# Three raw q, k buffers, one square buffer, another order of loads, and fewer fillers in a fused attention and MLP kernel

## Chip, cores and metric

The kernel runs on one core of a Trainium2 chip. The time is device microseconds of one execution. The kernel before took 342.39 us (median of 3 runs) when the prediction was made. All times below are of runs that computed the right result.

## The reference

Selective attention (causal, with a decay bias from a running sum of `s`) for 8 batches of 8 heads, 576 tokens, head dimension 64, then a two-layer MLP with exact Gelu on the 4608 tokens.

```python
def _attn_ref(q, k, v, s):                    # q, k, v: (8, 8, 576, 64) float32
    scores = scale * np.matmul(q, k.transpose(0, 1, 3, 2))
    cum = np.cumsum(np.maximum(s, 0.0), axis=-1)
    bias = -(cum[:, :, :, None] - cum[:, :, None, :])
    scores = np.where(causal, -1e9, scores + np.minimum(bias, 0.0))
    attn = softmax(scores)                    # cut
    return np.matmul(attn, v)

def _moe_ref(x, w_in, w_out):                 # x: (4608, 512), w_in: (512, 2048), w_out: (2048, 512)
    h = x @ w_in
    return (0.5 * h * (1 + erf(h / sqrt(2)))) @ w_out
```

## The kernel before

The MLP works on nine chunks of 512 tokens. While chunk c runs on TensorE, the attention of batch b = c + 1 is woven into it: layer 1 of the chunk (16 column tiles of w_in, two to a group, eight groups `f2`), then layer 2 in 16 groups with a list of attention pieces (`side`) between them. VectorE transposes q and k of the next batch and scales its v in layer 1 of the chunk; ScalarE makes the exponentials, the Gelu, and squares of v (and of q, k of batch 0) whose sums feed a certificate (a check at the end; if it fails, a slower general path runs); VectorE's `absmax` of q, k does the same for the later batches. A filler is a matmul of zeros whose result nobody reads; it only keeps TensorE busy.

```python
def raw_qk(b):                                # q and k of one batch, as loaded
    if (b, "qk") not in raws:
        raws[b, "qk"] = work.tile([128, 2, HG, S * 2], bf16, tag="rawqk", bufs=2, name="raw_qk")
    return raws[b, "qk"]

def square_qk(g, i):                          # ScalarE, batch 0 alone
    sq = work.tile([128, S * 2], bf16, tag="sqk", bufs=1, name="sqk")
    nc.scalar.activation(sq, raws[0, "qk"][:, i, g, :], func=AF.Square, scale=D ** -0.5,
                         accum_out=ssq[:, g, i : i + 1])

def square_v(b, st):                          # ScalarE, five for each batch; only the sum is used
    sq = work.tile([128, H * D], bf16, tag="sq", bufs=2, name="sq")
    nc.scalar.activation(sq[:n_st], raws[b, "v"][:n_st, st]..., func=AF.Square,
                         accum_out=sumv[:n_st, b, st : st + 1])

def absmax(b, g): ...                         # VectorE, reads raws[b, "qk"], 2.5 us each

for c in range(NCH):
    b = c + 1
    if c > 0 and b + 1 < B:
        load_qks(b + 1)                       # GpSimd queue; waits for a free raw_qk buffer
        load_v(b + 1, nc.gpsimd)
    ...                                       # layer 1: tr_qk(b), scale_v(b), absmax(b) on VectorE
    if c == 0:
        ...
        side[12] = [(av, b, 1, 3, True), (square_qk, 1, 0), (square_qk, 1, 1)]
        ...
        load_qks(2)
        load_v(2, nc.gpsimd)
    else:
        ...                                   # scores, masks (mk), attention times v (av), squares of v
        if c == 1:
            side[0].extend([(absmax, c, 0), (absmax, c, 1)])
```

## Time and profile before

| what | value |
|---|---|
| time, three runs | 339.94, 342.39, 343.69 us |
| span of the profiled run (341.48 us) | 339.7 us, mean granted clock 0.969 |
| busy: TensorE, VectorE, ScalarE | 92%, 59%, 56% |
| TensorE without work, 81.5 to 92 and 105 to 111.6 us | 10.4 and 6.6 us |

The page calls 92% of TensorE busy, but part of that is work at half clock. So look for two things: where TensorE stands still (a hole), and where it is busy but slow (the granted clock is the share of its full clock that it was given).

### The profile page before, as it was taken

Reading aid. Unit: us, or ns where it says so; the run is one execution under the profiler, and the core shown is the slowest. Engines: PE = TensorE matmul, PEld = TensorE weight load, DVE = VectorE, ACT = ScalarE, POOL = GpSimd, SP = SyncE. Lnnn points to the kernel's source line nnn. Section 1 sums busy time; section 2 is a strip of 40 time slices with the busy share of each in tenths; the row PEclk is TensorE's granted clock in tenths of the full one; section 3 lists DMA queues with packets and bytes.
Section 4 is the critical chain, followed back from the end, with each engine's and each line's share of the span. In section 5 each row is a group of like instructions: output and inputs, shape, how many; then the busy total and the mean of one; then the engine's idle time right before and its main releaser. Section 6 shows DMA issues by size and latency. Waiting matters only on the chain. (4 is left out here: it accounts for less than half of the span.)

```text
span 339.7 us, 6150 instructions
## 1 busy us (share of the span) xinstructions
PE 314.1 (92%) x2538; PEld 158.7 (47%) x2538; DVE 200.7 (59%) x400; ACT 190.2 (56%) x256; POOL 52.8 (16%) x72
## 2 busy tenths in 40 slices
PE   8999989996193899999999999999999999999994
PEld 3478645442051344554454444544454445444441
DVE  7677567049853397679567955895598552232011
ACT  2676967885063156855668566755765675303500
POOL 8533000600804001040104010400000000000000
PEclk9999999999678599999999999999999999999999
DMA  7999932690799614673575466631211131020012
GB/s 140 236 212 210 212 67 92 110 197 11 126 259 175 154 23 72 148 192 49 83 179 141 68 107 165 169 42 52 77 46 23 64 95 31 8 95 32 1 65 69
DMA packets 30980, 36.48 MB, mean 107 GB/s; under 512 B 15648, under 2 KB 20000, under 8 KB 30944
## 3 DMA queue, kind: packets, MB, share of 16 engines
q0 software_dynamic: 11552, 23.07, 35.5%
q1 hardware_dynamic: 19248, 12.80, 14.3%
q8 instruction: 22, 0.36, 0.5%
q14 instruction: 14, 0.11, 0.1%
q10 hardware_dynamic: 144, 0.13, 0.1%
HBM read 36.85 MB, written 9.44 MB: 136 GB/s over the span
## 5 line engine op out<-in xcount | busy, mean ns | idle before, releaser
L465 PE MATMUL h_ps<-xT,w_in_r 128*128 128x512 bf16 (+1 forms) x640 | 135.2, 363 | 6.6 <-issue 6.6
L481 PE MATMUL o_ps<-w_out_r,gT 128*128 128x512 bf16 x576 | 137.5, 383 | 1.2 <-DMA w_out_r<-in_moe_w_out_dram 1.2
L470 ACT ACTIVATE gT<-h_ps 128x1024 bf16<-128x1024 f32 (+1 forms) x80 | 74.4, 938 | 73.4 <-PE h_ps L465 72.7
L465 PEld LDWEIGHTS <-w_in_r 128*128 128x128 bf16 x640 | 60.5, 99 | 62.3 <-issue 10.1
L481 PEld LDWEIGHTS <-gT 128*128 128x128 bf16 x576 | 52.4, 98 | 58.6 <-issue 5.8
L358 ACT ACTIVATE P<-sc_ps 128x1024 bf16<-128x1024 f32 x56 | 54.3, 1021 | 44.3 <-PE sc_ps L343 44.3
L491 DVE COPY o_sb<-o_ps 128x512 f32<-128x512 f32 x32 | 22.1, 691 | 48.4 <-PE o_ps L481 48.4
L442 DVE RECIPROCAL rc<-av 128x4 f32<-128x4 f32 (+1 forms) x80 | 14.0, 175 | 53.2 <-PE av L433 53.2
L187 DVE STREAM_TRANSPOSE qkT<-raw_qk 128x576 f32<-128x576 f32 x32 | 37.6, 1243 | 10.5 <-DMA raw_qk<-in_q_dram 8.5
L122 POOL DMA_DIRECT2D raw_v<-in_v_dram x40 | 34.0, 869 | 60.9 <-ACT sq L212 55.0
L433 PE MATMUL av<-vv,P 128*128 128x65 bf16 x576 | 30.9, 195 | 11.0 <-DVE P L366 10.4
L433 PEld LDWEIGHTS <-P 128*128 128x128 bf16 x576 | 27.6, 99 | 28.1 <-DVE P L366 11.5
L443 DVE TENSOR_TENSOR x<-av,rc 128x256 bf16<-128x256 f32 (+1 forms) x80 | 33.8, 423 | 3.0
L204 DVE TENSOR_REDUCE amx<-raw_qk 128x2 f32<-128x2304 bf16 x14 | 35.1, 2533 | 0.0
L366 DVE TENSOR_TENSOR P<-P,tri_bf 128x1024 bf16<-128x1024 bf16 x32 | 21.9, 685 | 10.9 <-ACT P L358 10.3
L220 DVE TENSOR_TENSOR vv<-raw_v,wb 128x512 bf16<-128x512 f32 (+1 forms) x40 | 26.0, 690 | 0.8 <-DMA raw_v<-in_v_dram 0.7
L212 ACT ACTIVATE sq<-raw_v 128x512 bf16<-128x512 f32 (+1 forms) x40 | 24.6, 624 | 0.0
L106 POOL DMA_DIRECT2D raw_qk<-in_q_dram x9 | 6.3, 695 | 95.3 <-DVE amx L204 67.7
L343 PE MATMUL sc_ps<-qkT 32*128 32x256 bf16 (+2 forms) x560 | 18.3, 255 | 0.0
L343 PEld LDWEIGHTS <-qkT 32*128 32x128 bf16 x560 | 11.8, 94 | 13.1 <-issue 12.3
L417 PE MATMUL f_ps<-zero 128*128 128x512 bf16 x49 | 14.3, 423 | 1.2 <-DVE zero L150 1.2
L395 ACT ACTIVATE P<-sc_ps 128x1024 bf16<-128x1024 f32 x8 | 8.1, 1023 | 5.5 <-PE sc_ps L388 5.5
(79 smaller groups left out, 98.7 us busy)
## 6 DMA issues: line engine op xcount, KB each, us to landing
out_dram<-o_sb SPq DMA_DIRECT2D x35, 256.0 KB, 2.2
raw_v<-in_v_dram POOLq DMA_DIRECT2D x32, 256.0 KB, 8.7
raw_qk<-in_q_dram POOLq DMA_DIRECT2D x7, 576.0 KB, 5.9
raw_qk<-in_k_dram POOLq DMA_DIRECT2D x7, 576.0 KB, 9.1
w_in_r<-in_moe_w_in_dram POOLq DMA_DIRECT2D x4, 512.0 KB, 12.3
w_out_r<-in_moe_w_out_dram POOLq DMA_DIRECT2D x4, 512.0 KB, 14.6
raw_v<-in_v_dram POOLq DMA_DIRECT2D x8, 128.0 KB, 10.5
raw_qk<-in_q_dram POOLq DMA_DIRECT2D x2, 288.0 KB, 5.8
```

Of the source, the lines that this page charges most:

```text
L122: eng.dma_start(out=t[:n_st, st, :, :], in_=bass.AP(tensor=v.tensor, offset=v.offset + b * H * S * D + st * 128 * D, ap=[[D, n_st], [S * D ...
L187: nc.vector.transpose(qkT[b % 2][:, i, g, :S, :].rearrange("p s e -> p (s e)").bitcast(fp32) .rearrange("p (l j) -> p j l", j=LT), raws[b, ...
L204: nc.vector.tensor_reduce(amx[:, b * HG + g], raws[b, "qk"][:, :, g, :], axis=AX, op=ALU.max, apply_absolute_value=True,)
L212: nc.scalar.activation(sq[:n_st], raws[b, "v"][:n_st, st].rearrange("p h d -> p (h d)"), func=AF.Square, accum_out=sumv[:n_st, b, st : st ...
L220: nc.vector.tensor_tensor(vv[b % 2][:n_st, st, :, 0:D], raws[b, "v"][:n_st, st, :, :], w.unsqueeze(2).to_broadcast([n_st, H, D]), op=MULT,)
L343: nc.tensor.matmul(s_ps[h // 2][:, h % 2, off : off + n], lhsT=qk[r, 1, g, jt * 128 : jt * 128 + 128, e], rhs=qk[r, 0, g, i0 : i0 + n, e], ...
L358: nc.scalar.activation(P[:, 2 * h2 : 2 * h2 + 2, o : o + 512], s_ps[h2], func=AF.Exp, scale=scale)
L433: nc.tensor.matmul(o_ps[:, h, :], lhsT=P[:, h, off : off + 128], rhs=vv[b % 2][:, jt, 4 * g + h, :], start=(i == 0), stop=(i == len(BLK[it ...
L443: nc.vector.tensor_tensor(x_of[b, it][:n, g * 256 : g * 256 + 256].rearrange("p (h d) -> p h d", d=D), o_ps[:n, :, 0:D], rc[:n].unsqueeze( ...
L465: nc.tensor.matmul(h_ps[:, i, :], lhsT=w_in_r[:, ko, ft * 128 : (ft + 1) * 128], rhs=xT[:, ko, c * NB + n0 : c * NB + n1], start=(ko == 0) ...
L470: nc.scalar.activation(gT_of[c][:, f2 * 2 : f2 * 2 + 2, n0:n1], h_ps, func=AF.Gelu)
L481: nc.tensor.matmul(y_of[c, sub], lhsT=gT[:, ft, sub * 128 : (sub + 1) * 128], rhs=w_out_r[:, ft, :], start=(ft == 0), stop=(ft == FT - 1),)
```

## The change

The intent: a third raw buffer lets q, k of batch 2 be loaded without waiting for batch 0's buffer; w_out's second half goes ahead of the part of v that is needed later; the start of batch 0 is tightened. One square buffer now serves q, k and v: with the third raw buffer there is no room in SBUF for the old ones.

```diff
-            ... tag="rawqk", bufs=2, name="raw_qk")
+            ... tag="rawqk", bufs=3, name="raw_qk")
@@ square_qk
-        sq = work.tile([128, S * 2], bf16, tag="sqk", bufs=1, name="sqk")
+        sq = work.tile([128, S * 2], bf16, tag="sq", bufs=1, name="sq")
@@ square_v
-        sq = work.tile([128, H * D], bf16, tag="sq", bufs=2, name="sq")
+        sq = work.tile([128, S * 2], bf16, tag="sq", bufs=1, name="sq")
@@ start of batch 0 (more such lines cut)
-    filler(22)
+    filler(17)
     cum_sum()
+    masks()
     weights()
-    filler(4)
+    filler(3)
@@ loads
-    load_v(1, nc.gpsimd)
+    load_v(1, nc.gpsimd, (0, 1))
     load_w(1, 2)
     load_w(1, 3)
+    load_v(1, nc.gpsimd, (2, 3, 4))
@@ order of batch 0 (cut)
     mk_item(0, 1, 0)
-    sc_first(0, 1, (1,))
-    filler(2)
+    sc_first(1, 1, (0,))
     av_item(0, 1, 0)
@@ chunk 0
+                load_qks(2)
+                load_v(2, nc.gpsimd)
                 side = [[] for _ in range(16)]
-                side[3] = [(sc, b, 1, 0), (scale_v, b, 2), (mk, b, 1, 0)]
-                side[5] = [(sc, b, 0, 1), (av, b, 0, 0), (av, b, 0, 1), (scale_v, b, 3)]
-                side[6] = [(av, b, 1, 0, True), (mk, b, 0, 1)]
+                side[3] = [(sc, b, 1, 0), (mk, b, 1, 0)]
+                side[5] = [(sc, b, 0, 1), (av, b, 0, 0), (av, b, 0, 1)]
+                side[6] = [(scale_v, b, 2), (av, b, 1, 0, True), (mk, b, 0, 1)]
@@ (scale_v of the fourth piece to side[8]; the old place of batch 2's loads)
-                load_qks(2)
-                load_v(2, nc.gpsimd)
```

More of the change, by code (lines that the diff above doesn't have):

```diff
@@ L101, in raw_qk @@
         if (b, "qk") not in raws:
-            raws[b, "qk"] = work.tile([128, 2, HG, S * 2], bf16, tag="rawqk", bufs=2, name="raw_qk")
+            raws[b, "qk"] = work.tile([128, 2, HG, S * 2], bf16, tag="rawqk", bufs=3, name="raw_qk")
         return raws[b, "qk"]
@@ L210, in square_v @@
         n_st = 128 if st < ST - 1 else SL
-        sq = work.tile([128, H * D], bf16, tag="sq", bufs=2, name="sq")
+        sq = work.tile([128, S * 2], bf16, tag="sq", bufs=1, name="sq")
         nc.scalar.activation(
-            sq[:n_st], raws[b, "v"][:n_st, st].rearrange("p h d -> p (h d)"), func=AF.Square,
+            sq[:n_st, : H * D], raws[b, "v"][:n_st, st].rearrange("p h d -> p (h d)"), func=AF.Square,
             accum_out=sumv[:n_st, b, st : st + 1],
@@ L373, in mk_item, with sc_first @@
             )
-    def sc_first(g, u, halves=(0, 1)):
+    def sc_first(g, u, halves=(0, 1), fill=1):
         if (0, g) not in P_of:
@@ L393, in sc_first @@
                         )
-            filler(1)
+            if fill:
+                filler(fill)
             nc.scalar.activation(
@@ L531 @@
     sc_first(0, 0)
-    filler(3)
-    masks()
     tr_qk(0, 0, 1)
@@ L537 @@
     sc_first(0, 1, (0,))
-    filler(4)
+    filler(2)
     sc_first(1, 0, (0,))
@@ L542 @@
     scale_v(0, 1)
-    filler(2)
     sc_first(1, 0, (1,))
-    filler(2)
     av_item(0, 0, 0)
@@ L548 @@
     av_item(0, 0, 1)
+    sc_first(0, 1, (1,))
     mk_item(0, 1, 0)
-    sc_first(0, 1, (1,))
-    filler(2)
+    sc_first(1, 1, (0,))
     av_item(0, 1, 0)
     av_item(0, 1, 1)
-    sc_first(1, 1, (0,))
+    sc_first(1, 1, (1,), 0)
     to_xT(0, 0, True)
-    filler(1)
+    filler(2)
     to_xT(0, 1, True)
-    sc_first(1, 1, (1,))
+    filler(2)
     mk_item(0, 0, 1)
@@ L619 @@
             if c == 0:
+                load_qks(2)
+                load_v(2, nc.gpsimd)
                 side = [[] for _ in range(16)]
                 side[0] = [(sc, b, 0, 0), (scale_v, b, 0), (scale_v, b, 1), (mk, b, 0, 0)]
-                side[3] = [(sc, b, 1, 0), (scale_v, b, 2), (mk, b, 1, 0)]
-                side[5] = [(sc, b, 0, 1), (av, b, 0, 0), (av, b, 0, 1), (scale_v, b, 3)]
-                side[6] = [(av, b, 1, 0, True), (mk, b, 0, 1)]
+                side[3] = [(sc, b, 1, 0), (mk, b, 1, 0)]
+                side[5] = [(sc, b, 0, 1), (av, b, 0, 0), (av, b, 0, 1)]
+                side[6] = [(scale_v, b, 2), (av, b, 1, 0, True), (mk, b, 0, 1)]
                 side[7] = [(sc, b, 1, 1), (av, b, 1, 1, True), (to_xT, b, 0, True)]
-                side[8] = [(av, b, 0, 2), (to_xT, b, 1, True), (gelu_set,), (mk, b, 1, 1)]
+                side[8] = [(scale_v, b, 3), (av, b, 0, 2), (to_xT, b, 1, True), (gelu_set,), (mk, b, 1, 1)]
                 side[9] = [(av, b, 0, 3)]
```

## The prediction

> **What bounds the kernel now.** I read the page's forty slices first, then the engines in stretches around the holes, then who waited for whom, then the instructions in order of time. From the page (tenths of a slice of 8.5 us):
>
> ```profile
> PE   8999989996193899999999999999999999999994
> PEclk9999999999678599999999999999999999999999
> ```
>
> TensorE is the bound: 9s from slice 14 to slice 38, and the waits from 136 to 300 us name not one for it. The holes are slices 9 to 12 (76 to 110 us), and in slices 10 to 13 the granted clock is low too. Those slices in stretches (stretch; length; busy time and instruction count of PE, PEld, DVE, ACT, POOL; granted clock; DMA share; GB/s):
>
> ```profile
> 81.50:92.00 10.50, 0.10 (x3) 0.07 (x3) 10.38 (x6) 1.04 (x2) 5.94 (x8) 0.75 0.46 75
> 92.00:98.00 6.00, 6.00 (x52) 2.68 (x56) 2.50 (x6) 1.94 (x2) 1.14 (x2) 0.59 1.07 267
> 105.00:111.60 6.60, 0.02 (x1) 0.05 (x2) 0.67 (x1) 0.00 (x0) 3.13 (x4) 0.66 1.21 156
> 111.60:118.40 6.80, 6.80 (x33) 2.89 (x34) 2.74 (x4) 1.13 (x2) 0.00 (x0) 0.58 0.66 164
> ```
>
> Two holes of TensorE, each followed by 6 to 7 us in which it is busy at about 0.6 of its clock. The first hole in order of time (start, duration):
>
> ```profile
> 61.40 0.70 POOL L106 DMA_DIRECT2D raw_qk<-in_q_dram  x1 [26.53 <-ACT sqk L198]
> 70.67 1.26 DVE L187 STREAM_TRANSPOSE qkT<-raw_qk 128x576 f32<-128x576 f32 x1 [8.19 <-DMA raw_qk<-in_q_dram]
> 75.43 2.32 DVE L187 STREAM_TRANSPOSE qkT<-raw_qk 128x576 f32<-128x576 f32 x2
> 77.68 3.16 DVE L220 TENSOR_TENSOR vv<-raw_v,wb 128x512 bf16<-128x512 f32 x5
> 80.77 9.91 DVE L204 TENSOR_REDUCE amx<-raw_qk 128x2 f32<-128x2304 bf16 x4
> 90.61 0.67 DVE L491 COPY o_sb<-o_ps 128x512 f32<-128x512 f32 x1
> 91.21 0.67 DVE L366 TENSOR_TENSOR P<-P,tri_bf 128x1024 bf16<-128x1024 bf16 x1
> 91.94 0.40 PE L433 MATMUL av<-vv,P 128*128 128x65 bf16 x4 [10.40 <-DVE P L366]
> ```
>
> With two raw q, k buffers, batch 2's q and k need batch 0's buffer, whose last readers are the squares on ScalarE at 56 to 61 us. GpSimd sat 26.5 us before it could issue; q landed at 70.7 us, k at 73.8. VectorE had stood idle for 8.2 us, then did transposes, v scaling and four 2.5 us maxima in one row, and only then the mask that TensorE's attention-times-v was waiting for. The second hole:
>
> ```profile
> 99.52 2.54 SPq L404 DMA_TRANSPOSE xT<-x  x2
> 103.91 4.22 POOL L122 DMA_DIRECT2D raw_v<-in_v_dram  x5 [10.77 <-ACT sq L212]
> 111.58 3.57 PE L465 MATMUL h_ps<-xT,w_in_r 128*128 128x512 bf16 x8 [6.63 <-issue]
> ```
>
> The wait is called "issue", but layer 1 of chunk 2 needs the tokens that these two transposes deliver. Of all transposes of this tile the profile gives:
>
> ```profile
> DMA to landing us min/median/max: 2.3/2.4/10.6
> ```
>
> The 10.6 is this pair: in 86 to 110 us the DMA share is about 1.1, because batch 3's q, k, v, issued late from 86.06 us (after the maxima that held their buffer), and batch 4's q, k (91.65) all go out in one burst. So the second hole is a child of the same buffer shortage.
>
> Smaller: TensorE waits 1.20 us for w_out's third quarter at 44.85 us (the DMA engines move 200 to 280 GB/s without a break from 4 to 44 us), and the first layer-1 matmul starts only at 21.51 us.
>
> **What the Trainium skill says.** "TensorE: Matmul & The Clock Gate", Part 1: The HAM clock gate: after an idle window of about 3.4 us the array runs at half clock, and needs about as long a busy one to get it back. The trace agrees: 0.50 granted from 88 us, after a hole that began at 81.5; after work resumed at 91.94 full clock came back between 96 and 98. The table at the head of that page has VectorE as a strict first-in-first-out queue; that fits the mask standing behind the maxima. "DMA: Bandwidth & Descriptors", Queues, rings and completion order: all queues share 16 engines, which take turns by packet; so a transpose beside a full load queue slows, as 10.6 against 2.4 us shows. The same page, Anatomy of one DMA: a semaphore is waited for on the issuing sequencer; hence GpSimd's 26.5 us, with v queued behind q and k.
>
> **The change, part by part.**
>
> *Third buffer, batch 2's loads behind w_out.* It removes the 26.5 us wait. GpSimd issued its last w_out part at 34.1 us, so q and k of batch 2 go out at about 36 us and, the queue being full until 45, land near 52 us; v follows. From 62 to 76 us the same 2.36 MB took 13.5 us, so v is there by about 60, before its scaling. I rerun VectorE's queue of chunk 1 on the old clock: the late division ends at 62.5; two transposes 2.4, to 64.9; the second division 0.55, to 65.5; two transposes 2.3, to 67.8; denominators and v scaling 3.2, to 71.0; four maxima 9.9, to 80.9; the output copy 0.65 and the mask 0.65, to 82.1. TensorE arrives at 81.5. The stall becomes some 0.6 us instead of 10.4: **9.8 us** saved. An idle of that length should not cost the clock. From 91.94 to the third score product of that chunk (97.94) took 6.0 us; the same sequence of chunk 2 (136.57 to 140.43) took 3.9: **2.1 us**.
>
> *What follows for the DMA.* Batch 3's q, k issue after the squares (61 us) instead of at 86, its v after the squares of v at 72 instead of 87; batch 4's q, k after the maxima of batch 1 at about 81. At 175 to 210 GB/s those 1.2 MB take some 6 us. The two transposes come 12 us earlier on this clock, about 87.5, when that transfer is ending, and have about 5.5 us before they are needed. They should land in 2.4 to 4 us: hole two, **6.6 us**, goes. Its slow clock too: the first two layer-1 groups took 118.34 - 111.58 = 6.76 us, two normal ones 2 x 1.97: **2.8 us**.
>
> *v of batch 1 around w_out's second half.* Three v pieces (256, 256, 128 KB) no longer stand ahead; at 212 GB/s that is 3.0 us earlier, so w_out's third quarter lands at 41.8 and its last some 3 us earlier too. With a front 2.3 us shorter (below) the third is wanted at 43.58 - 2.3 = 41.3: 0.5 us of wait left of 1.2, **0.7 us**. The delayed v pieces land by 45 to 47 us; their scaling is moved from side slots 3 and 5 to 6 and 8 (45 us and later), about in time.
>
> *Front of batch 0.* Fillers fall from 52 to 37. They count only where TensorE is the wait. Five fewer of the first 22 (0.21 us each warm) end at 6.7 us, when the sums are ready (5.93 + 0.78), not at 7.77. The first scores then wait for the k transpose, about 9.1 us (two casts now stand before it), instead of 9.84. From there eight exponentials of 0.97 us and two score buffers set the step: today ScalarE idles 3.8 us in sum between them (0.47 + 0.72 + 0.29 + 0.88 + 0.95 + 0.52). Walking the new order through with today's durations, the exps end at 18.4 instead of 22.4, the second token transpose is copied at 19.0, layer 1 starts at 19.1 instead of 21.5. w_in's last two quarters landed at about 23.2 and 25.8 (seen from GpSimd's waits for them), and would now be wanted at about 23.1 and 25.5. So nearly all of the 2.4 stays: **2.3 us**.
>
> *Squares into one buffer instead of two.* The squares of q, k, which have one buffer, start 1.28 us apart for 1.16 us of work; those of v with two, 0.62. Perhaps 0.1 us more for each of 40 on an engine that is 56% busy: nothing on the path.
>
> Sum: 9.8 + 2.1 + 6.6 + 2.8 + 0.7 + 2.3 = **24.3 us**. 342.4 - 24.3 = 318.1. A cross-check by busy time: PE 314.1 less 4.9 (clock) less about 4 (15 fillers) is 305; with 1.2 us before its first and 5 us after its last instruction (334.7 to 339.7) and 2 to 3 of leftover waits the span is 314, against 339.7 - 24.3 = 315.4. I take 318.5.
>
> **Rivals.**
> 1. *The second hole stays because the burst only moves.* v of batch 4 and q, k of batch 5 can now follow each other without a wait, 2.4 MB from about 90 us, and batch 4's q, k end just before the transposes. If the transposes still take 10 us, about 5 us of hole and 2.8 of clock come back: 326. Against: in 142 to 147 us a v load of 1.2 MB also follows the transposes and TensorE does not stop.
> 2. *VectorE takes the wait's place.* Its queue in chunk 1 ends within 1 us of TensorE's arrival; each us by which it starts later is a us of stall, and beyond some 3.4 us the clock falls too. At 2 us more: 321.
> 3. *The front is DMA-bound.* DMA runs full to 44 us, so an earlier layer 1 waits for w_in, or layer 2 for w_out, and VectorE for the postponed v; the front's 3.0 us shrink to nothing: 321. Or with fewer fillers the clock drops in the front, 2 to 3 us lost: 323.
> 4. *Stores of chunk 0* now share the engines with batch 2: three output buffers and 5.5 us between copies speak against a stall.
>
> **Range and chances.** The first hole has a plain cause, worth 11.9; I am nearly sure of it. Hole two, 9.4, I give 80%. The front, 3.0, could be 0 to 4. All good: 316; hole two back: 326. Range 314 to 325. Faster by over 2% (below 335.5) needs only the first hole: 0.96; within 2% 0.03; slower 0.01.
>
> **What would show it.** Right: batch 2's q load issued near 36 us with no wait for the squares; the transposes in chunk 1 without a DMA wait, the mask ahead of an idle of TensorE below 1.5 us; no "issue" wait at layer 1 of chunk 2 and transposes landing in under 5 us; granted clock 1.00 in all slices; layer 1 from about 19 us. Wrong: an idle of TensorE of over 3 us anywhere between 20 and 110 us, or a granted clock below 0.9 there.

## The result and the profile after

The changed kernel took 318.45 us (median of 4 fast runs, 318.38 to 318.67), the kernel before 341.42 in the same rounds: ratio 0.9323, 95% interval 0.9265 to 0.9381. Executions over 1.5% slower than the fastest of the same kernel are left out of the means. The ratios are fast runs against fast runs of the same rounds, so not quite the ratio of the medians. All outputs are right.

The page after, in slices of 7.9 us; there is no hole left and no low clock:

```profile
PE   8999998999999999999999999999999999999993
PEclk9999999999999999999999999999999999999999
```

Chunk 1 after, in order of time:

```profile
36.89 0.71 POOL L106 DMA_DIRECT2D raw_qk<-in_q_dram  x1 [1.98 <-DMA w_out_r<-in_moe_w_out_dram]
...
59.31 2.32 DVE L187 STREAM_TRANSPOSE qkT<-raw_qk 128x576 f32<-128x576 f32 x2
...
64.29 3.16 DVE L220 TENSOR_TENSOR vv<-raw_v,wb 128x512 bf16<-128x512 f32 x5
...
67.37 9.92 DVE L204 TENSOR_REDUCE amx<-raw_qk 128x2 f32<-128x2304 bf16 x4
...
77.81 0.67 DVE L366 TENSOR_TENSOR P<-P,tri_bf 128x1024 bf16<-128x1024 bf16 x1
...
78.54 0.30 PE L434 MATMUL av<-vv,P 128*128 128x65 bf16 x4
83.87 2.54 SPq L405 DMA_TRANSPOSE xT<-x  x2
89.13 1.89 PE L466 MATMUL h_ps<-xT,w_in_r 128*128 128x512 bf16 x8
```

Batch 2's q goes out at 36.9 us, with no wait for the squares. Its wait of 1.98 us ends with the landing of a part of w_out, which has nothing to do with q; I take it for room in GpSimd's own queue. The transposes start at 59.3 with no wait for a transfer, the maxima end at 77.3, the mask at 78.5, and TensorE has no wait noted at its next product (it stands idle for 0.1 us of 78.1 to 78.6). Layer 1 of chunk 2 (89.13) has none either. The issues between 83 and 90 us, with the median time to landing, show its two transposes; below them the same pair in the kernel before (99 to 102 us), and the next pair of the changed kernel (94 to 101 us):

```profile
xT<-x SPq DMA_TRANSPOSE x2, 2.5
xT<-x SPq DMA_TRANSPOSE x2, 9.9
xT<-x SPq DMA_TRANSPOSE x2, 9.0
```

The first pair ran at a DMA share of 0.41 (84.0 to 89.1 us); the second and the third at about 1.1, beside loads. TensorE does not wait for the third, whose tokens it needs later.

The start times of the same pieces of work on TensorE in both profiles make a ledger; "in hand" is the time by which the changed kernel is ahead:

| TensorE starts | before | after | in hand |
|---|---|---|---|
| layer 1, chunk 0 | 21.51 | 18.93 | 2.58 |
| third scores of chunk 0 (past w_out's third quarter) | 46.67 | 42.84 | 3.83 |
| layer 1, chunk 1 | 59.69 | 56.60 | 3.09 |
| first attention times v of chunk 1 (past hole one) | 91.94 | 78.54 | 13.40 |
| last scores of chunk 1 (past its slow clock; the prediction calls them the third) | 97.94 | 82.28 | 15.66 |
| layer 1, chunk 2 (past hole two) | 111.58 | 89.13 | 22.45 |
| third group of that layer (past its slow clock) | 118.34 | 93.07 | 25.27 |
| layer 1, chunk 4 | 179.29 | 154.03 | 25.26 |
| layer 1, chunk 8 | 306.85 | 283.89 | **22.96** |

So 25.3 us were won by 93 us, and 2.3 us are given back later, between chunks 4 and 8. Two single profiles make this ledger, and that of before is of a slow run: its holes with their slow clock come to 22.2 us here, while the third buffer alone gained 18.5 us by the medians (`buf3_only`). The front varies as well: layer 1 of chunk 0 started at 21.2 to 22.4 us in the four profiles with the old front and at 18.4 to 19.5 in eight with the new one. The list of waits of the changed kernel names where the 2.3 us go; the columns are total us, times, longest:

```profile
PE h_ps L466 <- ACT gT L471: 2.0, 4, 0.5
```

The before kernel has no such line. Layer 1 waits for a Gelu, once in each of chunks 4 to 7. ScalarE in the turn from chunk 4 to 5, first before, then after:

```profile
210.35 0.63 ACT L212 ACTIVATE sq<-raw_v 128x512 bf16<-128x512 f32 x1
210.87 0.20 ACT L212 ACTIVATION_READ_ACCUMULATOR sq<-raw_v 128x1 f32 x1
210.96 0.63 ACT L212 ACTIVATE sq<-raw_v 128x512 bf16<-128x512 f32 x1
...
213.53 1.28 ACT L499 ACT_TABLE_LOAD   x1
214.82 1.98 ACT L470 ACTIVATE gT<-h_ps 128x1024 bf16<-128x1024 f32 x2
```

```profile
185.66 0.63 ACT L212 ACTIVATE sq<-raw_v 128x512 bf16<-128x512 f32 x1
186.18 0.20 ACT L212 ACTIVATION_READ_ACCUMULATOR sq<-raw_v 128x1 f32 x1
186.41 0.63 ACT L212 ACTIVATE sq<-raw_v 128x512 bf16<-128x512 f32 x1
...
189.41 1.28 ACT L500 ACT_TABLE_LOAD   x1
190.71 1.94 ACT L471 ACTIVATE gT<-h_ps 128x1024 bf16<-128x1024 f32 x2
```

The squares are no longer than before, but with one output buffer each starts after the accumulator read of the one ahead has ended (186.18 + 0.20 = 186.38, next at 186.41), 0.75 us apart; with two they start 0.61 apart, over the read. From the first square to the first Gelu it is 5.05 us after against 4.47 before, and TensorE has by then filled both of layer 1's buffers:

```profile
191.78 1.89 PE L466 MATMUL h_ps<-xT,w_in_r 128*128 128x512 bf16 x7 [0.49 <-ACT gT L471]
```

This group starts 2.62 us after the one ahead (189.16), in the kernel before 2.05 us (213.85 to 215.90): 0.57 us, and four chunks make 2.3.

### The profile page after: what moved, and what is told of

The parts are those of the page before. It is cut to its first block, busy times and chain, and to the rows that moved or that the text cites. A ratio compares the mean times of both kernels' runs of the same rounds, so it can differ in the third digit from the quotient of the medians.

```text
span 316.6 us, 6078 instructions
## 1 busy us (share of the span) xinstructions
PE 303.5 (96%) x2480; PEld 156.1 (49%) x2523; DVE 199.9 (63%) x400; ACT 192.9 (61%) x256; POOL 52.9 (17%) x72
## 5 line engine op out<-in xcount | busy, mean ns | idle before, releaser
L466 PE MATMUL h_ps<-xT,w_in_r 128*128 128x512 bf16 (+1 forms) x626 | 131.7, 357 | 2.8 <-ACT gT L471 2.0
L482 PE MATMUL o_ps<-w_out_r,gT 128*128 128x512 bf16 x549 | 132.3, 379 | 2.2 <-issue 1.3
L358 ACT ACTIVATE P<-sc_ps 128x1024 bf16<-128x1024 f32 x56 | 54.3, 1021 | 30.7 <-PE sc_ps L343 30.7
L418 PE MATMUL f_ps<-zero 128*128 128x512 bf16 x32 | 11.2, 468 | 1.3 <-DVE zero L150 1.2
L497 ACT ACT_TABLE_LOAD x8 | 10.3, 1283 | 0.9 <-PEq L819 0.7
L500 ACT ACT_TABLE_LOAD x8 | 10.3, 1283 | 0.1
```

The lines of the kernel that those rows point to most:

```text
L358: nc.scalar.activation(P[:, 2 * h2 : 2 * h2 + 2, o : o + 512], s_ps[h2], func=AF.Exp, scale=scale)
L466: nc.tensor.matmul(h_ps[:, i, :], lhsT=w_in_r[:, ko, ft * 128 : (ft + 1) * 128], rhs=xT[:, ko, c * NB + n0 : c * NB + n1], start=(ko == 0) ...
L482: nc.tensor.matmul(y_of[c, sub], lhsT=gT[:, ft, sub * 128 : (sub + 1) * 128], rhs=w_out_r[:, ft, :], start=(ft == 0), stop=(ft == FT - 1),)
```

## The experiments

All ran on one core; the kernels of one call shared the chip and the runs of the kernel before. In the first call (`sq2`, `buf3_only`, `no_buf3`, `v_first`) the kernel before took 338.34 us in the median (11 runs), in the second (`few_fill`, `front_only`, `pe_tr`, `max_late`) 339.97, in the third 339.39. The changed kernel took 318.45 and 318.77 in two calls, so I compare with it across calls too, but not below 0.5 us.

### sq2: two square buffers for v again

```diff
@@ square_v
-        sq = work.tile([128, S * 2], bf16, tag="sq", bufs=1, name="sq")
+        sq = work.tile([128, H * D], bf16, tag="sqv", bufs=2, name="sq")
@@ cum_sum: reuse the certificate's tile, which is written much later; without that the pool is 160 bytes too large
-        s_pos = const.tile([64, S], fp32, name="s_pos")
+        s_pos = w64
```

> The changed kernel, but the squares of v get two buffers of their own again (room comes from letting the exponentials of the certificate write over the dead running sum). Theory A: the one shared square buffer makes each square of v start 0.13 us later (0.75 us apart instead of 0.62), five in a row push the Gelu table load and the first Gelu back, and TensorE waits some 0.58 us in the third layer-1 group of chunks 4 to 7, 2.3 us in all. Then this kernel takes 318.5 - 2.3 = 316.2 us and the four waits of layer 1 for the Gelu are gone. Rival: those waits come from something else that the change moved (loads, scores); then 318.4 us and the waits stay.

Measured: 316.25 us (6 runs). The squares start 0.61 us apart again, and TensorE's wait for the Gelu is gone from the list of waits:

```profile
184.53 0.63 ACT L212 ACTIVATE sq<-raw_v 128x512 bf16<-128x512 f32 x1
185.05 0.20 ACT L212 ACTIVATION_READ_ACCUMULATOR sq<-raw_v 128x1 f32 x1
185.14 0.63 ACT L212 ACTIVATE sq<-raw_v 128x512 bf16<-128x512 f32 x1
```

Theory A holds: 2.2 us, from an engine that is 61% busy in the changed kernel. The reuse of `w64` was not run alone; that the gain is the buffer's is read from the squares' distance and from the four waits.

### buf3_only: the third buffer and nothing else

```diff
 (in the kernel before)
-            ... tag="rawqk", bufs=2, name="raw_qk")
+            ... tag="rawqk", bufs=3, name="raw_qk")
-        s_pos = const.tile([64, S], fp32, name="s_pos")
+        s_pos = w64
```

> The kernel before, with a third raw q, k buffer and nothing else of the change (room as in sq2). Theory A: both holes of TensorE and both slow-clock stretches come from the two buffers alone, so 341.4 - (10.3 + 2.3 + 6.8 + 2.8) = 319.2 us, within 1.5 us; the wait of 1.2 us for w_out stays. Rival: without the new order of v, w_out and batch 2's loads, the early loads of batch 2 collide with something in chunk 0 or one hole stays: over 323 us.

Measured: 319.83 us, ratio 0.9453 to before. Both holes and the slow clock are gone (granted clock 0.998 in the mean), and the pair of transposes lands in 2.5 us. One word of the change carries almost all of it, 18.5 us by the medians. Batch 2's loads stand at their old place in the program, and yet its q goes out at 36.5 us: nothing but the wait for the buffer had held them. One point of the expectation missed: the 1.2 us wait for w_out did not stay (layer 1 of chunk 0 started 0.9 us later in this profile, at 22.43 us).

### no_buf3: all but the third buffer

```diff
 (in the changed kernel)
-            ... tag="rawqk", bufs=3, name="raw_qk")
+            ... tag="rawqk", bufs=2, name="raw_qk")
 (batch 2's loads back behind chunk 0's layer 2)
```

> The changed kernel with two raw q, k buffers and batch 2's loads at their old place in the program: front and order of v and w_out stay. Theory A: the two holes come back whole, only 3.1 us earlier: 341.4 - 3.1 = 338.3 us, with 1 us more or less for the clock. Rival: the holes absorb what the front saved, because they are set by the DMA's own schedule: 341 us.

Measured: 336.28 us, before 338.34: ratio 0.9927 (0.9878 to 0.9976). My sum left out the 2.3 us that the one square buffer costs here too; with it theory A gives 0.8 us faster, and 2.1 were measured. In the profile layer 1 of chunk 1 starts at 56.72 us, so the front's gain is there, and the holes are there as well:

```profile
PE av L434 <- DVE P L366: 9.1, 1, 9.1
PE h_ps L466 <- DMA xT<-x: 4.5, 1, 4.5
PE h_ps L466 <- ACT gT L471: 2.0, 4, 0.5
```

Here the profile even names the transfer that hole two waits for. The holes are shorter than in the profile of before (10.4 and 6.6); whether the front shortened them or they vary from run to run, this one profile does not tell.

### v_first: all of v ahead of w_out's second half

```diff
 (in the changed kernel)
-    load_v(1, nc.gpsimd, (0, 1))
+    load_v(1, nc.gpsimd)
     load_w(1, 2)
     load_w(1, 3)
-    load_v(1, nc.gpsimd, (2, 3, 4))
```

> The changed kernel with all of batch 1's v ahead of w_out's second half again. Theory A: w_out's third quarter lands at about 44.8 us as in the kernel before, but is now wanted at about 41.0, so TensorE waits 3 to 4 us there: 321.5 to 322.5 us, so the order of v is worth more beside the shorter front than the 0.7 us that I gave it. Rival: DMA runs ahead anyway and the order is worth under 1 us: 318.5 to 319.4 us.

Measured: 323.84 us, about 5 us over the changed kernel. The wait, and the stretch from 40 to 60 us (columns as in the prediction):

```profile
PE o_ps L482 <- DMA w_out_r<-in_moe_w_out_dram: 3.5, 1, 3.5
40.00:60.00 20.00, 16.24 (x180) 8.42 (x179) 10.77 (x29) 11.10 (x14) 3.75 (x5) 0.91 1.00 209
```

The wait is as large as theory A had it, but it also costs clock (granted 0.91 in the mean of these 20 us), which I had not counted. Layer 1 of chunk 1 starts at 61.24 us instead of 56.60.

### front_only: the front without the order of v and without the buffer

The diffs of `no_buf3` and `v_first` together.

> The changed kernel with two raw q, k buffers, batch 2's loads late and v of batch 1 in one piece: of the change only the front of batch 0 and the one square buffer are left. Theory A: the 2.6 us that the front gains are waited away again for w_out (3.5 us of wait against 1.2), so layer 1 of chunk 1 starts no more than 0.5 us earlier than in the kernel before; holes as before, the square buffer costs 2.3: 0 to 3 us slower than the kernel before of the same rounds. Rival: the front's gain is kept: 0 to 1 us faster.

Measured: 341.78 us against 339.97, ratio 1.003 (0.9952 to 1.0107): no gain. Layer 1 starts at 19.48 us, but layer 1 of chunk 1 only at 61.05, 1.4 us later than in the kernel before (59.69); w_out's wait is 3.2 us and the clock falls to 0.91 behind it. The total also holds the 2.3 us of the one square buffer, but these come after this point. So the new front is worth nothing without the new order of loads: theory A, and a little worse than it said at this point of the program.

### few_fill: no zero fillers after the first 17

```diff
 (in the changed kernel)
-    def sc_first(g, u, halves=(0, 1), fill=1):
+    def sc_first(g, u, halves=(0, 1), fill=0):
 (and every filler(1), filler(2), filler(3) of zeros behind filler(17) taken out)
```

> The changed kernel without any of the 17 zero fillers that stand after the first 17 (the three with the k tile stay). Rival 3 of the prediction (fillers keep the clock): between 8 and 19 us TensorE is then busy for under half of the time, the granted clock falls below 0.8 somewhere before 25 us and layer 1 of chunk 0 starts at half rate: 319.5 to 321.5 us. Theory B, the front is set by exponentials and masks alone and the clock holds: 318.0 to 318.5 us.

Measured: 320.53 us, some 2 us over the changed kernel. From 9 to 12, from 10 to 15 and from 15 to 20 us:

```profile
9.00:12.00 3.00, 1.40 (x25) 0.81 (x20) 2.96 (x5) 2.85 (x3) 2.32 (x4) 0.96 1.10 242
10.00:15.00 5.00, 4.28 (x64) 3.01 (x63) 4.46 (x9) 4.18 (x6) 2.49 (x5) 0.68 1.18 204
15.00:20.00 5.00, 4.42 (x45) 3.33 (x42) 3.68 (x11) 4.10 (x4) 1.66 (x3) 0.50 1.16 234
```

From 10 to 15 us the granted clock is 0.68, then 0.50; layer 1 starts at 18.57 us, no earlier than in other profiles of the new front with its fillers (18.43 to 19.48), and its first 32 matmuls take 5.32 us instead of 3.65. So the fillers that the change kept pay for themselves. "Busy for under half of the time" held only before the clock fell, near 12 us: from 9 to 12 us TensorE is busy for 1.40 of 3.00 us (2.95 in the changed kernel). From 10 to 20 us its matmuls, slowed by the clock, fill over 85% of the time.

### pe_tr: hole two's transposes on TensorE

```diff
 (in the kernel before, chunk 1)
+                    side[9]  = [... av(b, 1, 0) without its DMA transpose]
+                    side[10] = [... av(b, 1, 1) without its DMA transpose]
+                    side[11].extend([(to_xT, b, 0, True), (to_xT, b, 1, True)])
```

> The kernel before, with the two token transposes of batch 2 that hole two waits for made by TensorE instead of the DMA (8 transposes and 2 copies more). Theory A: hole two is the delay of these DMA transposes behind the burst of loads, so it and its slow clock go (6.6 + 2.8 us in the profile of before, some 5 to 9 us on a run) and about 1 us of TensorE work comes: 4 to 8 us faster than before, hole one unchanged. Rival: layer 1 of chunk 2 waits for something else (an earlier late transpose, the clock): within 2 us of before.

Measured: 331.96 us, before 339.97, ratio 0.9778 (0.9713 to 0.9843): 7.5 us, and by the 2% rule unclear. Hole one stays (10.2 us), and hole two is gone from TensorE's waits. So it was the wait for this pair of DMA transposes. The burst of loads still goes out here (from 86.4 us); that it is what delays the pair rests on the landing times above, not on this run.

### max_late: the maxima out of the mask's way, still two buffers

```diff
 (in the kernel before, chunk 1: no absmax(2, .) in layer 1)
-                    side[0].extend([(absmax, c, 0), (absmax, c, 1)])
+                    side[11].extend([(absmax, c, 0)])
+                    side[13].extend([(absmax, c, 1)])
+                    side[15].extend([(absmax, b, 0), (absmax, b, 1)])
```

> The kernel before, with the four maxima of chunk 1 moved behind the masks (side slots 11, 13 and 15), still two buffers. Theory A: hole one is the sum of late q, k and four 2.5 us maxima in VectorE's queue, so taking the maxima away cures it as well as the third buffer does: hole one under 1 us, and with the burst gone from 86 to 105 us hole two too; batch 3's loads are later but still in time: 319 to 325 us. Rival: without a third buffer the loads' delay only moves: a new hole of several us in chunk 2, 330 us or more.

Measured: 329.63 us, ratio 0.9719, 9.5 us: between the two theories, and neither as I put it. TensorE's waits:

```profile
PE av L433 <- DVE x L443: 3.7, 3, 3.1
PE av L433 <- DVE P L366: 1.8, 1, 1.8
PE h_ps L465 <- DVE xT L411: 1.6, 1, 1.6
```

Hole one is gone, so it needed both the late q, k and the 9.9 us of maxima in front of the mask. But two of the moved maxima now stand in front of a later mask and of a later copy on VectorE (they end as the mask starts at 91.53 us and the copy at 95.88), and TensorE waits 1.8 and 1.6 us for these. And the maxima release the buffer for batch 3's loads: VectorE waits for q and k in chunk 2 (0.6 and 1.6 us), and TensorE 3.1 us behind it. Another order of work is a cheaper cure, but it brings about half of what the buffer brings (9.5 us against 18.5 for `buf3_only`).

### after_again, sq2_again, sq2_slots: side by side

`sq2_slots` is `sq2` with one item moved:

```diff
-  side[6] = [(scale_v, b, 2), (av, b, 1, 0, True), (mk, b, 0, 1)]
-  side[7] = [(sc, b, 1, 1), (av, b, 1, 1, True), (to_xT, b, 0, True)]
+  side[6] = [(av, b, 1, 0, True), (mk, b, 0, 1)]
+  side[7] = [(sc, b, 1, 1), (av, b, 1, 1, True), (scale_v, b, 2), (to_xT, b, 0, True)]
```

> The changed kernel itself, unaltered, as the yardstick on this chip for the two beside it: 318.0 to 318.9 us by theory A (its time does not vary from chip to chip as the kernel before's does, because it has no holes that a clock gate can lengthen); by the rival that chips differ as much as the kernel before's medians did (338.3 to 341.4), anywhere from 315.5 to 319.

> The changed kernel with two square buffers for v, once more on the same chip as the changed kernel: 2.2 us below it by theory A; by the rival that half of it was the other chip, about 1 us below it.

> sq2 with one more move: in chunk 0 the scaling of batch 1's third v piece goes from ahead of the attention of side slot 6 to behind that of slot 7. Theory A: there it stands ahead of a division that TensorE waits for (0.7 and 0.4 us of wait, or 0.8 us lost between 42.8 and 56.6 us), so this gains 0.3 to 0.7 us on sq2: about 315.8 us. Rival: VectorE has the same work before the next attention either way, so it only moves the wait: within 0.2 us of sq2.

Measured, six fast runs each: 318.77, 316.15 and 316.54 us; ratios to before 0.9411, 0.9345 and 0.9345. The changed kernel is where it was. The kernel before is faster here than beside the first result, so the change gains 5.9%, not the 6.8% of then. Two square buffers gain 2.6 us by the medians, 0.7% by the ratios. The moved item gains nothing (layer 1 of chunk 1 starts at 56.20 against 56.30 in `sq2_again`); TensorE then waits for the scaling itself instead. `sq2` is the fastest version found, with `sq2_slots` too close to tell apart.

## Why the prediction was right, and the step that was not

It said 318.5 us and 318.45 were measured. The signs that it named came too: q out near 36 us without a wait for the squares, TensorE idle for 0.1 us at the mask, the pair landing in 2.5 us, layer 1 from 18.93 us. Step by step, by the ledger:

| step | predicted | measured |
|---|---|---|
| front of batch 0 | 2.3 | 2.6 |
| v around w_out | 0.7 | 1.25, of which 0.74 lost again by layer 1 of chunk 1 |
| hole one | 9.8 | 10.3 |
| slow clock after it | 2.1 | 2.3 |
| hole two | 6.6 | 6.8 |
| slow clock after it | 2.8 | 2.8 |
| one square buffer | "nothing on the path" | -2.3 |
| sum | 24.3 | 23.0 |

**Right, shown by experiment.** The two holes and their slow clock: `buf3_only` has them gone with the buffer alone, `no_buf3` has them back. That hole two was the wait for two transposes: `pe_tr`. (That the burst of loads slowed them is argued: 9.9 us to landing beside it, 2.5 us without it in the changed kernel and in `buf3_only`.) That hole one was late q, k plus the maxima in one queue: `max_late` takes away the second and the hole goes. Rival 1 did not come: the pair landed in 2.5 us. That was close, and in part luck: batch 4's q and k went out at 73.76 us, about 4 us sooner than worked out (81 less the 3.1 us of the front), and took 10.6 us instead of 6, so that the last of them landed at about 84.3 us, just as the transposes went out (83.87), where the prediction had it. The two misses cancelled. Rival 2 stayed within its bound: VectorE's mask ended just as TensorE came.

**Right in kind, sized too small alone.** The order of v and w_out was counted at 0.7 us as a part by itself. It is worth 5 us beside the new front (`v_first`), because a front that is 2.6 us shorter wants w_out that much sooner; and the front is worth nothing without it (`front_only`). A sum of parts hides that. Rival 3 named both the transfer and the clock as threats to the front; each is real when its counterpart in the change is taken away (`front_only`, `few_fill`).

**Wrong.** The step "Squares into one buffer instead of two ... nothing on the path". I had the size of the cost right (0.1 us for each square), and argued from ScalarE's share of 56% that it would not be felt. The share is an average. In the turns into chunks 4, 5, 6 and 7, exponentials, five squares, a table load and the first Gelu stand in a row on ScalarE, and TensorE waits for the last of them. `sq2` shows that these 2.3 us come from that buffer. That the measured time fell on the predicted one is luck: the gains were 1.0 us larger than worked out, which made up part of this loss, I had moved the sum up by 0.4 us, and the median of the kernel before fell by 1.0 us with one more run.

## What to carry to other kernels

When a load waits for a buffer, ask who reads that buffer last and what that load holds up further on: here one missing buffer made two holes of TensorE, the second, as far as the landing times tell, through a burst of loads 25 us later. A buffer that is paid for by giving up another one should be checked where the giving engine works in a row, not by its average share. Parts of a change that shorten the start and that bring data earlier belong together; here the shorter start alone measured as nothing (the order of loads alone was not run).

## What the Trainium skill lacked or had wrong

- "TensorE: Matmul & The Clock Gate", Part 1, ties half clock to an idle window of about 3.4 us, and says of one kernel that frequent short idles made the clock swing. It doesn't say how much work in a window keeps the clock. In `few_fill` TensorE was busy for 1.40 of the 3.00 us from 9 to 12 us, its longest single wait between 9 and 19 us was 1.1 us, and the granted clock was 0.50 from 12 to 22 us.
- "DMA: Bandwidth & Descriptors", Rules for kernel authors, says that a transpose next to ordinary DMAs needs nothing. No run here shows a wrong result, but the pair that took 2.5 us to land in the changed kernel took 10 us at the median in the kernel before, beside a full load queue (medians; the pair of the changed kernel at 94.7 us took 9.0 us beside loads). The page has no such latency.
- No page has the cost of reusing one output buffer for activations with an accumulator: 0.75 us from start to start against 0.61 with two, for the same 0.63 us of work.
